# Linear attention into a top-1 mixture of experts on one core: five edits of a hand-written instruction order

## The chip, the cores and the metric

The kernel runs on one core of one Trainium2 chip. The metric is the device time of one execution in microseconds (us). Five engines take instructions from queues of their own, each in program order: TensorE (PE, with its weight loads shown apart as PEld), VectorE (DVE), ScalarE (ACT), GpSimd (POOL) and SyncE (SP), which mostly issues DMAs. An engine waits on semaphores for what another engine or a DMA has made.

## The reference

What is computed, cut to its core (B=4, H=8, S=768, D=48; 3072 tokens of 384; 8 experts, F=1024):

```python
for t in range(S):                                    # per batch and head, state 48x48
    cur = einsum('bhd,bhe->bhde', u * k_t, v_t)
    y[:, :, t] = einsum('bhd,bhde->bhe', r_t, state + cur)
    state = w * state + einsum('bhd,bhe->bhde', k_t, v_t)
x = y as (3072, 384)
logits = x @ w_gate + modality_bias[modality_id]      # 384 x 8
e_idx = argmax(logits); gate_w = softmax(logits)[e_idx]
for e in range(8):
    out[e_idx == e] = gate_w * (relu(x[e_idx == e] @ w1[e]) @ w2[e])
```

Inputs and outputs are float32.

## The kernel before, in words

**Attention in 24 units.** The recurrence is computed in chunks of 128 tokens. A unit is one chunk of one batch: 6 chunks outside, 4 batches inside, so unit i+4 carries on the state of unit i. For a unit, with transposed (`rT`, `kT`) and plain (`r`, `k`, `v`) inputs, the engines do:

- VectorE: `kc` = kT times powers of the decay (`keys`, L400).
- GpSimd: `rc` = rT times powers (`decay`, L376), `rk` = rc*kc for the bonus term (`own_keys`, L393; from unit 14 on `ru` = r*k*u instead, L389 and L390), `kt` = k times its weight (`carry`, L383).
- TensorE: scores `psc` (L450), bonus (L414), values `py` (L478, L485, L513), new states `pst` (L496, L500). VectorE masks the scores into `at` (L456) and makes the diagonal part `dv` (L427).
- VectorE or ScalarE add the state up (`st`, L550, L552), and both make the token's row in two half-precision parts (L535, L562, L566). SyncE turns the row with a transposing DMA (`flip`, L571) for the router's matmuls.

In unit i, the keys, scores and carries of units ahead are made beside the values of unit i and the rows of unit i-1.

**Routing.** Units are routed in groups of four (later three and two). When a group's places are known, GpSimd writes each of its units' rows to the array `rows` in memory, sorted by expert, with an indirect DMA (`send`, L680, each with a tiny memset L679 ahead of it). Three groups are sent from units 13, 17 and 21, four DMAs in a stretch; the first group is sent one DMA at a time between other GpSimd work of unit 9.

**First expert slots inside the attention.** One expert is known ahead, and its rows are worked on in slots of 128 rows while the attention still runs. For slot k: `s_turn(k)` has SyncE load a row number into a register, read 128 sorted rows with a transposing DMA into one half of `mxT` (L1024) and their gate factors into `mt` (L1025); `s_up(k)` is 72 matmuls (L1037), `s_high` and `s_low` split the relu in two parts `hh` (ScalarE, L1041) and `hl` (VectorE, L1046), `s_down` is 16 matmuls on `hh` (L1111) and 8 on `hl` (L1116), `s_due` (VectorE, L1096) makes the row factors. The expert's weights stand as a coarse half `whi` and a fine half `wlo`; `fine(q)` (VectorE, L977) makes 1024 columns of `wlo`. L1111 takes four terms with `whi`, four with `wlo`, and so on; `fine(5)` makes the columns of the last three. The weights' two scales are undone by the product `wf` (`undo`, L963). Slot 0 goes up in unit 12 and down in unit 13, slot 5 goes up in unit 22, and slots 6 to 9 in the tail, which starts behind unit 22. After it a device loop takes the remaining expert jobs.

**What sets the order.** Nothing schedules this kernel: each engine runs in the order in which `run()` is written. `plan(i, f)` puts f at the end of unit i, `soon(i, f)` into its middle; `ahead`, `turns` and `ups` are tables by unit; `route(i, d, f)` calls f for a group whose last unit was i-d. `first` holds for the units of the first form, up to unit 11.

Of the kernel before, what the change touches and what calls it, by code (L numbers as in the profile page):

```python
# [14 lines left out]
AF = mybir.ActivationFunctionType  # L15
# [4 lines left out]
B, H, S, D = 4, 8, 768, 48  # L20
# [46 lines left out]
class _Kernel:  # L67
# [16 lines left out]
    def setup(self):  # L84

        nc, c = self.nc, self.c
# [103 lines left out]
        self.scores(1)  # L190
        self.causal(0, 0)
        self.causal(0, 1)
        self.carry(0)
        self.own_keys(1)
        self.decay(2)
        pst = self.ps_s.tile([P, 512], F32, tag="s", name="psd")
        self.bonus(0, pst)
# [776 lines left out]
    def fine(self, q, part=0, parts=1):  # L974

        sl, sc = self.piece(q, part, parts)
        self.nc.vector.scalar_tensor_tensor(self.wlo[:, sl], self.raw[:, sl], sc, self.whi[:, sl], ALU.mult, ALU.subtract)  # L977
# [146 lines left out]
    def run(self):  # L1124
        nc, tc, m = self.nc, self.tc, self.m
# [25 lines left out]
        def plan(step, f):  # L1151
            at.setdefault(step, []).append(f)

        def piece(e, q, after=None):
            if q == 0:
                self.eid = nc.sync.value_load(self.ctl[:, e : e + 1], min_val=0, max_val=E - 1)
            self.load(self.eid, NQ, q, after=after)
# [3 lines left out]
        def scales(key, half, step, then=lambda: None):  # L1161
            def ask():
                begun[key] = self.scales_(key, slice(half, half + 1), self.ps_a, "big")
                next(begun[key])

            self.amid.setdefault(step, []).append(ask)
            plan(step, lambda: (run(begun[key], 9), then()))

        def chain(*gs):
            for g in gs:  # L1170
                yield from g
# [14 lines left out]
        fine = lambda q: lambda: self.fine(q)  # L1186
# [10 lines left out]
            plan(i, second(q))  # L1197
            plan(i + 3, norm(q))
        scales("w1", 0, 6)
        scales("w2", 1, 10, self.undo)  # L1200
        for q, i in enumerate((7, 8, 9)):
            soon(i, wide(q))
            plan(i, fine(q))
# [2 lines left out]
        plan(11, fine(3))  # L1206
        plan(12, wide(5))
        plan(12, fine(4))
        plan(12, fine(5))
        ahead = {0: (0, 1), 4: (2, 3), 8: (4, 5), 12: (6, 7), 16: (8,), 19: (9,)}  # L1210
        turns = {10: (0,), 11: (1,), 14: (2,), 15: (3,), 18: (4,), 19: (5,), 22: (6,)}
        ups = {12: 0, 14: 1, 16: 2, 18: 3, 20: 4, 22: 5}
        live = lambda i: 0 <= i < NU

        def route(i, d, f, *args):
            for lo, hi in GROUPS:
                if hi - 1 + d == i and lo in groups:
                    f(groups[lo], *args)

        def each(i, *fs):  # L1220
            for f in fs:
                if live(i):
                    f(i)


        def fill(n=1):
            if n < 99:
                n = min(n, quota.get(i, n))
                if i in quota:
                    quota[i] -= n  # L1230
            while n and fills:
                g = fills.pop(0)
                if next(g, fills) is not fills:
                    fills.append(g)
                    n -= 1

        quota = {1: 6, 2: 6, 3: 4}
        for i in range(NU - 1):
            if i > NEAR:
                each(i + 4, self.lines)  # L1240
            if i:
                each(i + 1, self.scores)
            if 0 <= i - 2 <= TURNED:
                self.flip(i - 2, False)
            route(i, 3, lambda u: fills.append(self.choose(u)))
            route(i, 5, lambda u: fills.append(chain(self.place(u), self.ahead(ahead[u["lo"]], u["pr"]))))
            up, down = ups.get(i), ups.get(i - 1)
            if down is not None:
                self.s_high(down, 0)
            first = i <= BARE  # L1250
            self.token(i - 1) if i else None
            for j in range(2 if first else 0):
                each(i - 1, lambda i: self.state(i, j))
                fill()
            if first:
                for f in early.get(i, ()):
                    f()
                gate = self.taken(i)
                if i <= NEAR:
                    self.lines(i + 3, gate if i else None)  # L1260
                fill()
            if first:
                each(i + 2, self.keys)
                for _ in self.factor(i - 1) if i else ():
                    fill()
                gate = self.causal(i + 1, 0)
                if i <= NEAR:
                    self.turned(i + 4, gate if i else None)
                fill()
                each(i - 1, self.high)  # L1270
                if 0 <= i - 2 <= TURNED:
                    self.flipped(i - 2)
                if i <= NEAR:
                    self.other(i + 4)
                else:
                    self.turned(i + 5, both=True)
                each(i + 1, lambda i: self.causal(i, 1))
                fill()
                gate = self.low(i - 1) if i else None
                for q in first_at.get(i, ()):  # L1280
                    piece(0, q, gate)
            if down is not None:
                self.s_high(down, 1)
            if ups.get(i - 2) is not None:
                self.s_take(ups[i - 2])
            if i and i - 1 == self.grp["lo"]:
                groups[i - 1] = self.grp
            fill()
            each(i, self.taken) if not first else None
            for j in range(0 if first else 2):  # L1290
                each(i - 1, lambda i: self.state(i, j))
                fill()
            for f in () if first else early.get(i, ()):
                f()
            if down is not None:
                self.s_low(down, 0)
                self.s_low(down, 1)
                self.s_due(down)
            late = i >= NU - 3
            if not first:  # L1300
                each(i + 2, self.keys)
                each(i + 5, lambda i: self.turned(i, both=True))
            for f in (lambda: each(i + 2, self.own_keys), lambda: each(i + 3, self.decay), lambda: None):
                if first:
                    route(i, 6, self.send, 1, True)
                f()
            if ups.get(i - 2) is not None:
                self.s_give(ups[i - 2])
            if not first:
                route(i, 6, self.send, B, True)  # L1310
            each(i + 2, self.carry)
            if first:
                route(i, 6, self.send, 1, True)
            route(i, 4, self.sign)
            if not first:
                for _ in self.factor(i - 1):
                    fill()
                self.own(i, 0)
                each(i - 1, self.high)
                for j in range(2):  # L1320
                    each(i + 1, lambda i: self.causal(i, j))
                    fill()
                self.own(i, 1)
                each(i - 1, self.low)
                fill()
            if i - 1 > TURNED:
                self.flip(i - 1)
            if i == NEAR:
                self.lines(i + 4)
                self.turned(i + 5, both=True)  # L1330
            fill()
            self.values(i)
            for g in range(2):
                if up is not None:
                    self.s_up(up, g)
                if down is not None:
                    self.s_down(down, g)
            for p in range(2):
                for h in range(2):
                    c, r = divmod(i + 1 - 2 * p - h, B)  # L1340
                    if r == 0 and 0 < c < NCH - 1 and not self.early(c):
                        self.fade(c, slice(2 * p, 2 * p + 2), range(2 * h, 2 * h + 2))
            if any(hi - 1 + d == i for lo, hi in GROUPS for d in (4, 5)):
                fill(99)
            route(i, 2, self.logits)
            route(i, 4, self.count)
            if late:
                route(i, 5, self.send, B, True)
            for f in at.get(i, ()):
                f()  # L1350
            for k in turns.get(i, ()):
                self.s_turn(k)
# [3 lines left out]
        i, j = NU - 2, NU - 1  # L1356
# [241 lines left out]
```

## Time and profile before

| | |
|---|---|
| median of 3 runs | 357.91 us (351.15, 357.91, 361.53) |
| profiled execution | 350.87 us, its span 349.0 us, mean granted TensorE clock 0.984 of full speed |
| PE, PEld | busy 328.6 us (94% of the span), 262.3 us (75%) |
| DVE | 222.6 us (64%) |
| ACT | 161.7 us (46%) |
| POOL | 168.0 us (48%) |
| memory | 50.29 MB in DMA packets, mean 144 GB/s |

The span runs from the first to the last instruction; 350.87 - 349.0 = 1.87 us lie around it. PE is busy nearly all the time, and POOL's 48% is an average: it is close to full in the first half of the span and nearly empty in the second. Times in the rows further down are microseconds from the span's start.

### The profile page before, as it was taken

The page shows a single profiled execution, that of the slowest core. Times are in us where ns is not written, and L with a number is a line of the kernel's source. Part 1 is how long each engine was busy: PE and PEld are TensorE (multiplying, and loading weights), DVE is VectorE, ACT ScalarE, POOL GpSimd, SP SyncE. Part 2 cuts the span into 40 slices and gives each one's busy share as a digit, 9 for nine tenths or more (in the row PEclk, how much of TensorE's full clock was granted, in tenths as well). Part 3 has the DMA queues.
Part 4 walks back from the last instruction along what each step waited for, and adds up shares of the span by engine and source line. Part 5 has one row for each costly group of instructions (what it writes and reads, how often), then busy time and mean ns, then how long its engine had stood idle before and what let it go on. Part 6 is the DMA issues. An engine that isn't in the chain of part 4 may idle for free. (4 is left out here: it accounts for less than half of the span.)

```text
span 349.0 us, 14765 instructions
## 1 busy us (share of the span) xinstructions
PE 328.6 (94%) x5387; PEld 262.3 (75%) x5387; DVE 222.6 (64%) x744; ACT 161.7 (46%) x379; POOL 168.0 (48%) x251
## 2 busy tenths in 40 slices
PE   7899999989898989998799999999999999999992
PEld 3687878779696959786778777777788888777771
DVE  6879688999786948696635863349333344337950
ACT  5756676755364547456433432256222222226920
POOL 8897688779985988375421631111111211111311
PEclk9989999999999998999899999999999999999999
DMA  7978989778999997814578541117832112111110
GB/s 136 268 177 237 238 233 243 211 208 169 269 237 186 253 255 149 182 50 139 130 158 258 198 115 48 45 45 220 214 67 46 45 45 65 48 45 45 36 45 5
DMA packets 51773, 50.29 MB, mean 144 GB/s; under 512 B 39176, under 2 KB 44041, under 8 KB 51472
## 3 DMA queue, kind: packets, MB, share of 16 engines
q1 hardware_dynamic: 47568, 37.45, 48.0%
q0 software_dynamic: 3200, 9.47, 7.9%
q10 hardware_dynamic: 960, 2.75, 3.1%
q8 instruction: 31, 0.51, 0.6%
q14 instruction: 14, 0.11, 0.1%
HBM read 30.55 MB, written 11.63 MB: 121 GB/s over the span
## 5 line engine op out<-in xcount | busy, mean ns | idle before, releaser
L1037 PEld LDWEIGHTS <-whi 128*128 128x128 f16 x1248 | 73.1, 98 | 5.2 <-DMA mxT<-rows 2.3
L1111 PEld LDWEIGHTS <-hh 128*128 128x128 f16 x416 | 38.4, 98 | 28.2 <-ACT hh L1041 3.5
L1037 PE MATMUL phb<-mxT,whi 128*128 128x128 f16 x720 | 47.5, 219 | 0.0
L1041 ACT ACTIVATE hh<-phb 128x256 f16<-128x256 f32 (+1 forms) x45 | 20.4, 454 | 43.5 <-PE phb L1037 17.9
L1037 PEld LDWEIGHTS <-wlo 128*128 128x128 f16 x624 | 38.3, 99 | 0.0
L376 POOL TENSOR_TENSOR rc<-ud,powr 128x512 f32<-128x512 f32 (+1 forms) x27 | 33.0, 1230 | 3.0 <-DMA ud<-in_pd 2.7
L680 POOL DMA_INDIRECT rows<-row,posi x24 | 25.3, 1056 | 16.4 <-issue 10.6
L456 DVE TENSOR_TENSOR at<-psc,mask 128x512 f32<-128x512 f32 x48 | 31.5, 681 | 2.6 <-remote 2.6
L1037 PE MATMUL phs<-mxT,whi 128*128 128x128 f16 x480 | 31.1, 222 | 2.0 <-DMA mxT<-rows 2.0
L1046 DVE SCALAR_TENSOR_TENSOR hl<-phb,hh 128x256 f16<-128x256 f32 (+1 forms) x45 | 22.7, 512 | 14.6 <-ACTq L1540 7.3
L450 PE MATMUL psc<-rc,kc 48*64 48x128 f32 x768 | 29.3, 278 | 2.7 <-issue 2.0
L1116 PEld LDWEIGHTS <-hl 128*128 128x128 f16 x208 | 19.9, 98 | 15.6 <-issue 2.8
L1006 POOL TENSOR_TENSOR seenb<-otb,putb 128x1 int32<-128x1 int32 x15 | 3.7, 249 | 56.9 <-ACTq L1520 49.5
L485 PE MATMUL py<-kv,at 128*64 128x48 f32 x768 | 28.5, 227 | 0.9 <-issue 0.6
L1111 PE MATMUL po<-whi,hh 128*128 128x384 f16 x128 | 28.8, 327 | 0.1
L1111 PE MATMUL po<-wlo,hh 128*128 128x384 f16 x128 | 28.6, 326 | 0.1
L485 PEld LDWEIGHTS py<-kv,at 128*64 128x64 f32 x768 | 26.8, 144 | 1.7 <-issue 1.0
L562 ACT ACTIVATE row<-py,sx 128x384 f16<-128x384 f32 x24 | 14.0, 582 | 29.6 <-DVE sx L329 26.5
L1037 PE MATMUL phb<-mxT,wlo 128*128 128x128 f16 x360 | 27.4, 219 | 0.0
L450 PEld LDWEIGHTS psc<-rc,kc 48*64 48x64 f32 x768 | 22.0, 133 | 6.5 <-issue 3.0
L1116 PE MATMUL po<-whi,hl 128*128 128x384 f16 x128 | 23.4, 326 | 1.2 <-PEq L1594 1.1
L997 ACT ACTIVATE otb<-po,fac 128x384 f32<-128x384 f32 x15 | 8.7, 582 | 34.1 <-PE phb L1037 30.8
(273 smaller groups left out, 651.3 us busy)
## 6 DMA issues: line engine op xcount, KB each, us to landing
ud<-in_pd SPq DMA_DIRECT2D x34, 192.0 KB
raw<-in_w SPq DMA_DIRECT2D x12, 512.0 KB
kv<-in_pt SPq DMA_DIRECT2D x10, 576.0 KB
kv<-in_pt SPq DMA_DIRECT2D x14, 384.0 KB
raw<-in_w SPq DMA_DIRECT2D x2, 1536.0 KB, 7.4
ud<-in_pd ACTq DMA_DIRECT2D x14, 192.0 KB
rows<-pad SPq DMA_DIRECT2D x1, 1544.0 KB
rows<-row,posi POOLq DMA_INDIRECT x24, 4.0
```

The costliest lines, as they stand in the source:

```text
L376: nc.gpsimd.tensor_mul(u["rc"][:, s], u["rT"][:, s], self.powr[:, s])
L450: nc.tensor.matmul(u["ps"][j][s, pr * P : (pr + 1) * P], u["kc"][r, pr, s], u["rc"][r, pr, :], start=True, stop=True)
L456: return nc.vector.tensor_mul(u["at"][:, j * NPR : (j + 1) * NPR, :], u["ps"][j].rearrange("p (q t) -> p q t", q=NPR), self.mask.unsqueeze ...
L485: nc.tensor.matmul(py[t, sl], u["at"][:, j * NPR + pr, t], u["v"][:, sl], start=c == h == 0, stop=h == H - 1 and i >= JOINED, skip_group_c ...
L562: self.nc.scalar.activation(u["x16"][:, :DM], u["x"], AF.Copy, scale=u["g"]["sx"][:, b : b + 1])
L680: i = nc.gpsimd.indirect_dma_start(out=self.rows, out_offset=bass.IndirectOffsetOnAxis(ap=u["posi"][:, b : b + 1], axis=0), in_=u["row"][: ...
L997: self.nc.scalar.activation(ot, po[:, :DM], AF.Copy, scale=gf[:, t : t + 1])
L1037: self.nc.tensor.matmul(ph[:, q * P : (q + 1) * P], w[:, c0 : c0 + P], self.xT[:, xq, t * P : (t + 1) * P], start=i == q == 0, stop=i == l ...
L1041: self.nc.scalar.activation(self.hh[:, f0 : f0 + fb, t * P : (t + 1) * P], p3, AF.Relu)
L1046: self.nc.vector.scalar_tensor_tensor(self.hl[:, f0 : f0 + fb, r], p3, 0.0, self.hh[:, f0 : f0 + fb, r], ALU.max, ALU.subtract)
L1111: self.nc.tensor.matmul(po[:, :DM], self.hh[:, f, t * P : (t + 1) * P], w[:, c0 : c0 + DM], start=n == 0, stop=False)
L1116: self.nc.tensor.matmul(po[:, :DM], self.hl[:, f, t * P : (t + 1) * P], self.whi[:, c0 : c0 + DM], start=False, stop=f == FB - 1)
```

## The change

Five edits of the order; what is computed stays the same.

1. In the setup `own_keys(1)` comes ahead of `carry(0)`.
2. The product `wf` at the end of unit 10 is made by ScalarE (an activation with a scale) instead of VectorE. The same product for later experts stays with VectorE.
3. `fine(5)` moves from the end of unit 12 to unit 13, behind `s_low(0)` and `s_due(0)`.
4. In the units of the second form the four sends of a group come behind `own_keys` and ahead of `decay`, instead of behind `decay`. In units of the first form the order stays.
5. `s_turn(6)` is called at the end of unit 21 instead of unit 22.

```diff
@@ setup
         self.causal(0, 1)
+        self.own_keys(1)
         self.carry(0)
-        self.own_keys(1)
         self.decay(2)
@@ run()
         scales("w1", 0, 6)
-        scales("w2", 1, 10, self.undo)
+        scales("w2", 1, 10, lambda: nc.scalar.activation(self.wf, self.winv[:, 0:1], AF.Copy, scale=self.winv[:, 1:2]))
...
         plan(12, fine(4))
-        plan(12, fine(5))
...
-        turns = {10: (0,), 11: (1,), 14: (2,), 15: (3,), 18: (4,), 19: (5,), 22: (6,)}
+        turns = {10: (0,), 11: (1,), 14: (2,), 15: (3,), 18: (4,), 19: (5,), 21: (6,)}
...
                 self.s_due(down)
+                if down == 0:
+                    fine(5)()
...
-            for f in (lambda: each(i + 2, self.own_keys), lambda: each(i + 3, self.decay), lambda: None):
-                if first:
-                    route(i, 6, self.send, 1, True)
-                f()
+            if first:
+                route(i, 6, self.send, 1, True)
+            each(i + 2, self.own_keys)
+            route(i, 6, self.send, 1 if first else B, True)
+            each(i + 3, self.decay)
             if ups.get(i - 2) is not None:
                 self.s_give(ups[i - 2])
-            if not first:
-                route(i, 6, self.send, B, True)
+            if first:
+                route(i, 6, self.send, 1, True)
             each(i + 2, self.carry)
```

On GpSimd at the end of the setup (`rk` of unit 1, `kt` of unit 0, then `rc` of unit 2 and `kt` of unit 1):

```order
 L182 TENSOR_TENSOR uw<-w,uT 48x4 x2
+L393 TENSOR_TENSOR rk_274<-rc_198,kc_196 128x512
 L383 TENSOR_TENSOR kt_89<-kv_111,wtok 128x384
-L393 TENSOR_TENSOR rk_275<-rc_198,kc_196 128x512
 L376 TENSOR_TENSOR rc_277<-ud_87,powr 128x512
 L383 TENSOR_TENSOR kt_90<-kv_114,wtok 128x384
```

The product for unit 1's bonus now stands ahead of the one that uses `kv`, a tile of unit 0's plain inputs.

On VectorE at the end of unit 12 and in unit 13 (the second `wlo` piece is `fine(5)`; `dv`, `st`, `hl` are unit 12's and slot 0's):

```order
 L814 TENSOR_TENSOR lim<-pr_1418,steps 128x2
-L977 SCALAR_TENSOR_TENSOR wlo<-raw,ws,whi 128x1024 x2
+L977 SCALAR_TENSOR_TENSOR wlo<-raw,ws,whi 128x1024
 L520 TENSOR_TENSOR py_1780<-py_1780,dv_1746 128x384
...
 L1096 TENSOR_SCALAR fac<-mt_301,wf 128x1
 L1097 TENSOR_TENSOR ids<-mt_301,skip 128x1
+L977 SCALAR_TENSOR_TENSOR wlo<-raw,ws,whi 128x1024
 L400 TENSOR_TENSOR kc_1945<-ud_88,powk 128x512
```

The piece moved past `py`, `dv`, two state updates and slot 0's relu, and stands ahead of unit 15's keys.

On SyncE at the end of units 21 and 22 (the three transposes are the flips of units 19, 20 and 21; `ctl` is read for slot 6):

```order
-L571 DMA_TRANSPOSE xT_3131<-row_3130 128x6x128 x3
+L571 DMA_TRANSPOSE xT_3131<-row_3130 128x6x128 x2
 L1068 TENSOR_LOAD ctl
 L1068 ISA x2
...
 L1025 ISA
 L1025 DMA mt_301<-rows 128x4
+L571 DMA_TRANSPOSE xT_3131<-row_3130 128x6x128
 L1068 TENSOR_LOAD ctl
 L1068 ISA x2
```

The load of slot 6's rows now stands ahead of unit 21's flip instead of behind it.

## Rows read from the trace of the kernel before

**Rows 1.** Waits of TensorE: what, for what; us in total, times, longest us.

```profile
PE phs L1037 <- DMA mxT<-rows: 2.0, 1, 2.0
PE psc L450 <- issue: 2.0, 3, 1.0
```

**Rows 2.** Stretches: us; busy us of PE, PEld, DVE, ACT, POOL; granted clock; DMA.

```profile
17.30:20.40 3.10, 3.10 (x50) 2.28 (x48) 2.27 (x9) 1.61 (x4) 3.10 (x3) 0.50 1.00 220
80.00:100.00 20.00, 18.51 (x402) 16.12 (x399) 17.36 (x52) 8.54 (x21) 17.99 (x21) 1.00 1.06 238
129.98:133.20 3.22, 3.22 (x55) 2.91 (x49) 3.13 (x13) 1.60 (x5) 2.83 (x3) 0.50 1.05 284
170.96:174.83 3.87, 3.87 (x47) 3.67 (x46) 2.82 (x12) 0.58 (x1) 3.37 (x18) 0.56 0.71 204
```

**Rows 3.** GpSimd at the setup's end: start, us, operation [idle before, releaser].

```profile
11.90 1.01 POOL L383 TENSOR_TENSOR kt<-kv,wtok 128x384 f32<-128x384 f32 x1 [1.32 <-DMA kv<-in_pt]
12.87 1.72 POOL L393 TENSOR_TENSOR rk<-rc,kc 128x512 f32<-128x512 f32 x1
14.55 1.26 POOL L376 TENSOR_TENSOR rc<-ud,powr 128x512 f32<-128x512 f32 x1
```

**Rows 4.** VectorE and TensorE in the same stretch.

```profile
7.87 0.69 DVE L400 TENSOR_TENSOR kc<-ud,powk 128x512 f32<-128x512 f32 x1 [0.60 <-DMA ud<-in_pd]
12.59 0.86 DVE L400 TENSOR_TENSOR kc<-ud,powk 128x512 f32<-128x512 f32 x1 [0.21 <-DMA ud<-in_pd]
13.47 0.56 PE L500 MATMUL pst<-kv,kt 128*48 128x48 f32 x16
14.64 0.63 PE L414 MATMUL pst<-uw,rk 112*64 112x2 f32 x16 [0.61 <-POOL rk L393]
15.86 1.10 PE L450 MATMUL psc<-rc,kc 48*64 48x128 f32 x32 [0.59 <-POOL rc L376]
```

**Rows 5.** VectorE, GpSimd and TensorE in unit 10.

```profile
70.49 3.50 DVE L963 TENSOR_TENSOR wf<-winv 128x1 f32<-128x1 f32 x1
72.97 1.00 POOL L383 TENSOR_TENSOR kt<-kv,wtok 128x384 f32<-128x384 f32 x1
74.94 0.87 PE L513 MATMUL py<-dv,id 128*64 128x384 f32 x4 [0.54 <-DVE dv L427]
```

**Rows 6.** All of line 963: min/median/max ns, first and last start.

```profile
L963 DVE TENSOR_TENSOR wf<-winv x3: 159/161/3502, 70.5 to 327.8; 128x1 f32<-128x1 f32 x3
```

**Rows 7.** VectorE, GpSimd and TensorE in units 12 and 13.

```profile
84.72 3.28 DVE L977 SCALAR_TENSOR_TENSOR wlo<-raw,ws,whi 128x1024 f16<-128x1024 f32 x2
89.60 1.29 DVE L1046 SCALAR_TENSOR_TENSOR hl<-phs,hh 128x512 f16<-128x512 f32 x2
89.71 0.56 PE L500 MATMUL pst<-kv,kt 128*48 128x48 f32 x16 [0.81 <-DVE st L550]
90.34 0.81 PE L1111 MATMUL pos<-whi,hh 128*128 128x384 f16 x4
88.83 1.27 POOL L376 TENSOR_TENSOR rc<-ud,powr 128x512 f32<-128x512 f32 x1
94.16 0.96 POOL L680 DMA_INDIRECT rows<-row,posi  x1 [0.23 <-issue]
```

**Rows 8.** SyncE, GpSimd and TensorE from unit 21's sends to the tail.

```profile
158.44 7.94 SPq L571 DMA_TRANSPOSE xT<-row  x2
159.90 0.96 POOL L680 DMA_INDIRECT rows<-row,posi  x1 [0.23 <-issue]
167.52 1.24 SPq L1024 DMA_TRANSPOSE mxT<-rows  x1
170.46 2.35 PE L1037 MATMUL phs<-mxT,whi 128*128 128x128 f16 x24 [2.05 <-DMA mxT<-rows]
```

**Rows 9.** All of line 680, and how long its DMAs take to land.

```profile
L680 POOLq EVENT_SEMAPHORE  x4: 17/30/7572, 56.7 to 196.8; - x4
DMA to landing us min/median/max: 2.9/4.0/6.8
```

## The prediction

> **What bounds the kernel now.** TensorE is busy 328.6 of 349.0 us, so the first view is not who is busiest but what TensorE waits for. Its list of waits [rows 1] is headed by 2.0 us for the load of a slot's rows, and by 2.0 us in three pieces that stand under "issue", in which nothing that the profile shows was missing. The rest is a dozen waits under 1 us each. The timelines then say where four of them lie: two at the end of the setup [rows 4], one in unit 10 [rows 5], one in unit 13 [rows 7], and the 2.05 us at the start of the tail [rows 8]. The windows add what such an idle time does afterwards: behind three stands of TensorE there is a stretch in which it is busy all the time at a granted clock of 0.50 to 0.56, the lower of its two levels [rows 2]: 3.10 us at 0.50, 3.22 us at 0.50, 3.87 us at 0.56. Work that takes 3.87 us at 0.56 takes 3.87 x 0.56 = 2.17 us at full clock, so that stretch lost 1.70 us; the other two lost 1.55 and 1.61. In 80 to 100 us GpSimd is busy 17.99 of 20 us [rows 2]: there its queue has about 2.0 us of slack. Behind the attention it is nearly idle, and TensorE alone sets the end, so a wait of TensorE that goes is a gain in full unless something later takes it back.
>
> **Edit 1, the setup.** GpSimd sits idle for 1.32 us until 11.90, waiting for `kv` [rows 3]. `rk` of unit 1, now in front, needs no `kv`: its `kc` was done at 7.87 + 0.69 = 8.56 [rows 4]. It took 1.72 us beside a `kc` of VectorE that itself took 0.86 instead of 0.69; if the two are served one after the other, 0.46 of the 1.72 is the overlap (12.87 to 13.33, start of `rk` to near the end of that `kc`), and alone it takes 1.26. It fits the idle time: 10.58 to about 11.85. `kt` stays at 11.90 to 12.91, before TensorE uses it at 13.47. Then unit 2's `kc` (0.69) and `rc` (1.26) run one behind the other and end at 12.91 + 0.69 + 1.26 = 14.86, instead of 15.81. The bonus need not wait its 0.61 us, and the scores start at 14.85 instead of 15.86: **gain 1.01 us**. Bounds: if `kc` and `rc` overlap freely, 1.20; if VectorE's `kc` loses against three GpSimd products in a row, as in unit 10 below, scores no sooner and 0.2 us lost at the next masks, so -0.2. Of the clock stretch at 17.30 to 20.40 I take nothing in the forecast, because GpSimd stays only just ahead there; if the clock stays up, 1.55 us more.
>
> By the Trainium skill, page "SBUF — State Buffer", section "Who interferes with whom", a VectorE instruction with two inputs in SBUF and a GpSimd instruction that reads SBUF exclude each other for a whole instruction. The 1.72 beside 0.86 agrees [rows 3, 4]; by that rule the gain is 1.01, without it 1.20.
>
> **Edit 2, the product of scales.** VectorE's `wf` stood 3.50 us from 70.49 [rows 5]; the two other executions of the line took about 0.16 us [rows 6]. It ended only when GpSimd's third product in a row ended, at 72.97 + 1.00 = 73.97. TensorE then waited 0.54 us for `dv` behind it [rows 5]. On ScalarE the product takes about as little (0.16 is VectorE's own price; no row has ScalarE's), and what stands behind it there has slack of over 1 us. **Gain 0.54 us**; low end -0.1, if ScalarE's wait for the scales delays the row behind it. High end 0.54, since TensorE waited no longer. VectorE gets 3.3 us free; late next is unit 12's `kc`, which reads two tiles in SBUF as `wf` did and may stand in its place, but `dv` is ahead of it.
>
> By the same section of the Trainium skill the lock holds for the one instruction that has it. One GpSimd product (1.28 us) and the own 0.16 would make 1.44; 3.50 over three products speaks against that [rows 5], and the measurement decides. It is why I keep a starved `kc` among the rivals.
>
> **Edit 3, the last fine piece.** Two pieces took 3.28 us from 84.72 [rows 7], 1.64 each. TensorE's state matmuls waited 0.81 us for `st` at 88.9 to 89.71, behind them. Without the second piece `st` is there at about 89.57 - 1.64 = 87.9, ahead of TensorE: **gain 0.81 us**. The piece then starts behind slot 0's relu, which took 1.29 us from 89.60 [rows 7]. What stands ahead of that relu moves up by the same 1.64, so it can run from 87.96 to 89.25; with 0.2 us for two small instructions the piece runs from 89.5 to 91.1. The first matmul that wants it is the 14th of L1111; four of these take 0.65 us from one row to the next, 0.162 each; they start at 90.34 - 0.81 = 89.53 without the wait, and the 14th comes at 89.53 + 13 x 0.162 = 91.6. Half a microsecond to spare. Low end: if the relu doesn't come sooner, the piece ends at 89.60 + 1.29 + 0.2 + 1.64 = 92.7, 1.1 late, and the gain is -0.3. High end 0.81.
>
> **Edit 4, the sends.** At unit 13 `rc` stood at 88.83 to 90.10, the four sends behind it until 94.16 + 0.96 = 95.12 [rows 7]: 5.02 us. Now the sends start 1.27 us sooner and `rc` 5.02 us later. It is made three units ahead and its scores are computed one unit ahead, so it has about two units; from the state matmuls at 13.47 [rows 4] to those at 89.71 [rows 7] thirteen units pass, 5.9 us each, so 11.7 us of cover against 5.0. Nobody waits for rows sent 1.27 us sooner except slot 6's load (edit 5), and at unit 21 there is no `rc` left, so nothing moves there. **0 us**. What I can't price is the stands under "issue" that follow the sends of units 13, 17 and 21: 2.0 us in three pieces [rows 1] and 1.61 us of clock behind the longest. They may shrink or move with the sends: -1 to +1.6 us, taken as 0.
>
> **Edit 5, slot 6's rows.** The load started at 167.52 [rows 8], 1.14 us behind the end of the two flips at 158.44 + 7.94 = 166.38, and TensorE had its rows 170.46 - 167.52 = 2.94 us later. TensorE was free at 170.46 - 2.05 = 168.41. Asked for ahead of unit 21's flip, the load waits for the last of unit 21's sends: issued at 159.90, landing after 2.9, 4.0 or 6.8 us (least, median, most) [rows 9]. Rows are there 2.94 us behind that: at 165.7, 166.8 or 169.6. Wanted at 168.41, so at the median the wait of 2.05 is gone, and with it, I take it, the 1.70 us of low clock right behind it [rows 2]: **gain 3.75 us**. Low end: at 6.8 there is 1.2 us of wait and the low clock left, gain 0.8. Queued behind the waiting load on SyncE is unit 21's flip, up to 2 us later; the router wants it only behind slot 6's matmuls and unit 22's values.
>
> **Sum.** 1.01 + 0.54 + 0.81 + 0 + 3.75 = 6.11 us. Against the profiled execution's 350.87 that is 344.8 (-1.7%). That execution is as fast as the best of the three runs (351.15); their median is 357.91. For the time I start between the two, at 354.4: **348.3 us**.
>
> **Rivals.**
> 1. *More: the clock stays up at the start too.* TensorE reaches its first long stretch without the 1.2 us of waits [rows 4], and 1.55 us at 17.30 to 20.40 come on top: 343.2 (-2.2%). For it: the stretch lies right behind those waits. Against: some wait for GpSimd's next products remains.
> 2. *The load is asked sooner, but comes no sooner*, so that edit 5 doesn't do what it says: it waits for sends that land after 6.8 us. Sum 6.11 - 2.93 = 3.2, time 347.7 (-0.9%). For it: the slowest landing is in the trace [rows 9], and the memory is busy there. Against: the median.
> 3. *A starved `kc`* in the setup or in unit 12, as `wf` was: edit 1 at -0.2, time 346.0. GpSimd's products in a row speak for it, the 0.86 us of the `kc` at 12.59 against [rows 4].
> 4. *Slower: sends stand at the head of GpSimd's queue.* One stand of a send there took 7.57 us [rows 9]. If at units 13 and 17 the sends, now ahead, wait that long for something `rc` used to cover, `rc`, `kt` and `ru` stand behind them; with 2.0 us of slack each costs 5.6, and 1.6 of clock [rows 2]. 350.87 - 6.1 + 2 x 7.2 = 359.1 (+2.3%). It decides where the stand passes the slack. Against: the present sends start with only 0.15 to 0.23 us of idle time ahead of them, so they were ready.
>
> **How the numbers follow.** Chances: forecast 0.42, rival 1 0.28, rival 2 0.18, rival 3 0.07, rival 4 0.05. About 2%, 7 us, is what measurements of this kernel tell from no change, its three runs being 10 us apart. Faster by over 2%: rival 1 and the forecast's upper edge, 0.28 + 0.05 = 0.33; slower by over 2%: 0.05; within 2%: 0.62. The range: rival 1 with 1 us from the stands behind sends, 342; rival 2 from the runs' median, 357.91 - 3.2 = 354.7, with 1.3 of the stands, 356.
>
> **What would show it.** In the changed profile: the bonus at the setup's end starts without waiting, and the clock at 17 to 20 us tells forecast from rival 1; no 3.5 us instruction of VectorE in unit 10; the state matmuls in unit 13 without a wait, and no gap ahead of the 14th of L1111; slot 6's load ahead of unit 21's flip, its matmuls at about 166 us without a wait and at full clock. I am wrong if TensorE's waits go and the span doesn't shrink with them, if new stands under "issue" take their place, or if GpSimd shows a wait ahead of a send at unit 13 or 17.

## The result, and the profile after

The changed kernel took 352.22 us (median of 20 runs, 347.12 to 356.27) against 356.04 for the kernel before (20 runs, 351.06 to 361.53): **ratio 0.9891, 95% interval 0.9844 to 0.9938**, so 3.9 us faster (2.2 to 5.6) where 6.1 was forecast. The time lies inside the range of 342 to 356.

Ratios here are formed from the runs within 1.5% of the fastest of the same kernel, medians from all runs; the first profiled execution of the changed kernel (354.71 us, mean clock 0.966) lies outside, so the rows here are from a later one, the run `e1_all_again`: span 347.2 us, clock 0.989, against 349.0 and 0.984 before.

TensorE at the end of the setup and near 27 us (start, us, operation [idle before, releaser]):

```profile
13.90 0.63 PE L414 MATMUL pst<-uw,rk 112*64 112x2 f32 x16
14.73 1.10 PE L450 MATMUL psc<-rc,kc 48*64 48x128 f32 x32 [0.21 <-POOL rc L376]
...
24.18 1.22 PE L450 MATMUL psc<-rc,kc 48*64 48x128 f32 x32 [0.95 <-POOL kt L383]
26.41 0.33 PE L576 MATMUL pt<-id,row 128*128 128x128 f16 x3 [1.01 <-DVE at L456]
26.94 0.34 PE L576 MATMUL pt<-id,row 128*128 128x128 f16 x3 [0.20 <-DVE row0f L767]
```

The bonus no longer waits and unit 2's scores start at 14.73 instead of 15.86 [rows 4]; 14.85 was forecast. But 10 us later TensorE waits 0.95 us for GpSimd and 1.01 and 0.20 us for VectorE.

The product of scales, now on ScalarE, then SyncE around slot 6's load:

```profile
69.70 0.29 ACT L1200 ACTIVATE wf<-winv 128x1 f32<-128x1 f32 x1 [1.12 <-DVE winv L332]
```

```profile
146.98 9.75 SPq L571 DMA_TRANSPOSE xT<-row  x2
160.27 1.24 SPq L1024 DMA_TRANSPOSE mxT<-rows  x1
161.71 0.42 SPq L1025 DMA_DIRECT2D mt<-rows  x1
162.24 1.95 SPq L571 DMA_TRANSPOSE xT<-row  x1
```

The 3.50 us of VectorE [rows 5] are gone, and slot 6's load stands ahead of unit 21's flip. TensorE there:

```profile
165.30 0.22 PE L646 MATMUL pr<-oh,warm 128*128 128x8 f16 x3
165.38 1.50 PE L1037 MATMUL phs<-mxT,whi 128*128 128x128 f16 x24
...
169.99 0.34 PE L485 MATMUL py<-kv,at 128*64 128x48 f32 x4 [0.48 <-issue]
171.46 0.20 PE L485 MATMUL py<-kv,at 128*64 128x48 f32 x1 [1.14 <-issue]
171.59 1.15 PE L1111 MATMUL pos<-whi,hh 128*128 128x384 f16 x4
172.54 1.48 PE L1111 MATMUL pos<-wlo,hh 128*128 128x384 f16 x4
...
177.18 1.50 PE L1037 MATMUL phs<-mxT,whi 128*128 128x128 f16 x24
```

Slot 6's matmuls start at once, at full clock (24 in 1.50 us instead of 2.35 [rows 8]). Then come two stands, idle times of TensorE under "issue", of 0.48 and 1.14 us, which the first profile of the kernel before did not have, and low clock behind them: the eight L1111 shown end at 174.02, 2.4 us after their start, where full clock makes it 1.5 (four in 0.65 us [rows 7], the last ending 0.81 behind its row's start). Windows (us; busy of PE, PEld, DVE, ACT, POOL; clock; DMA) of the start, around unit 18 and of this stretch:

```profile
17.30:20.40 3.10, 3.10 (x76) 2.69 (x73) 2.92 (x13) 2.08 (x6) 3.10 (x3) 1.00 1.02 236
120.00:135.00 15.00, 14.16 (x242) 11.94 (x241) 10.27 (x33) 8.81 (x27) 13.43 (x18) 0.89 0.93 231
160.00:176.00 16.00, 13.98 (x206) 11.30 (x206) 9.99 (x36) 6.73 (x20) 4.47 (x20) 0.89 0.58 128
```

The clock at the start is 1.00 here, 0.50 in the kernel before [rows 2].

### The profile page after: what moved, and what is told of

The parts are those of the page before. It is cut to its first block, busy times and chain, and to the rows that moved or that the text cites. A ratio compares the mean times of both kernels' runs of the same rounds, so it can differ in the third digit from the quotient of the medians.

```text
span 351.9 us, 14762 instructions
## 1 busy us (share of the span) xinstructions
PE 331.9 (94%) x5387; PEld 265.1 (75%) x5387; DVE 220.9 (63%) x743; ACT 161.6 (46%) x380; POOL 165.8 (47%) x251
## 5 line engine op out<-in xcount | busy, mean ns | idle before, releaser
L1037 PEld LDWEIGHTS <-whi 128*128 128x128 f16 x1248 | 72.3, 98 | 5.4 <-issue 1.8
L1111 PEld LDWEIGHTS <-hh 128*128 128x128 f16 x416 | 38.5, 98 | 26.3 <-ACT hh L1041 3.1
L1037 PE MATMUL phb<-mxT,whi 128*128 128x128 f16 x720 | 47.5, 219 | 1.5 <-DVE mxT L1480 1.5
L1037 PEld LDWEIGHTS <-wlo 128*128 128x128 f16 x624 | 37.7, 98 | 0.5 <-issue 0.5
L376 POOL TENSOR_TENSOR rc<-ud,powr 128x512 f32<-128x512 f32 (+1 forms) x27 | 34.0, 1265 | 2.3 <-DMA ud<-in_pd 2.2
L485 PE MATMUL py<-kv,at 128*64 128x48 f32 x768 | 30.5, 232 | 2.8 <-issue 2.6
L1116 PEld LDWEIGHTS <-hl 128*128 128x128 f16 x208 | 19.9, 98 | 15.6 <-issue 2.8
L485 PEld LDWEIGHTS py<-kv,at 128*64 128x64 f32 x768 | 28.3, 148 | 4.0 <-issue 3.7
L1037 PE MATMUL phs<-mxT,whi 128*128 128x128 f16 x480 | 30.1, 219 | 0.7 <-DMA mxT<-rows 0.7
L1006 POOL TENSOR_TENSOR seenb<-otb,putb 128x1 int32<-128x1 int32 x15 | 2.9, 192 | 56.2 <-ACTq L1522 48.3
L1111 PE MATMUL po<-whi,hh 128*128 128x384 f16 x128 | 28.8, 327 | 0.0
L1111 PE MATMUL po<-wlo,hh 128*128 128x384 f16 x128 | 28.7, 326 | 0.0
L1037 PE MATMUL phb<-mxT,wlo 128*128 128x128 f16 x360 | 27.4, 219 | 0.0
L450 PEld LDWEIGHTS psc<-rc,kc 48*64 48x64 f32 x768 | 22.8, 141 | 4.2 <-POOL rc L376 1.9
```

The lines of the kernel that those rows point to most:

```text
L376: nc.gpsimd.tensor_mul(u["rc"][:, s], u["rT"][:, s], self.powr[:, s])
L450: nc.tensor.matmul(u["ps"][j][s, pr * P : (pr + 1) * P], u["kc"][r, pr, s], u["rc"][r, pr, :], start=True, stop=True)
L485: nc.tensor.matmul(py[t, sl], u["at"][:, j * NPR + pr, t], u["v"][:, sl], start=c == h == 0, stop=h == H - 1 and i >= JOINED, skip_group_c ...
L1037: self.nc.tensor.matmul(ph[:, q * P : (q + 1) * P], w[:, c0 : c0 + P], self.xT[:, xq, t * P : (t + 1) * P], start=i == q == 0, stop=i == l ...
L1111: self.nc.tensor.matmul(po[:, :DM], self.hh[:, f, t * P : (t + 1) * P], w[:, c0 : c0 + DM], start=n == 0, stop=False)
L1116: self.nc.tensor.matmul(po[:, :DM], self.hl[:, f, t * P : (t + 1) * P], self.whi[:, c0 : c0 + DM], start=False, stop=f == FB - 1)
```

## The experiments

Executions of one kernel lie 10 us and more apart, so edits worth 1 us don't show in a time. But TensorE runs the same instructions in the same order in every kernel here, so stretches of its timeline can be compared directly. Three are used:

- **S1**: from the span's start to the last three row transposes (L576) near 27 us.
- **S2**: from the first L1037 of slot 2 to the first of slot 3 (units 16 to 18, with unit 17's sends inside).
- **S3**: from the last router matmul ahead of slot 6 (L646) to the first L1037 of slot 6's second half (before: 168.20 to 179.80).

S1, S2 and S3 are each of one execution. The medians (us) are of all runs, of this kernel and of the kernel before on the same chip.

| kernel (edits in it) | ratio, 95% interval | medians | S1 | S2 | S3 |
|---|---|---|---|---|---|
| before (none) | | | 27.07 | 18.65 | 11.60 |
| e5_before_again (none) | one execution | 349.69 / 356.58 | 26.44 | 18.62 | 10.68 |
| e6_setup_only (1) | 1.0059, 0.9990 to 1.0129 | 354.75 / 356.58 | 26.96 | 16.80 | 12.02 |
| e10_wf_and_fine (2, 3) | 0.9960, 0.9850 to 1.0070 | 355.40 / 357.82 | 26.79 | 17.20 | 11.88 |
| e4_sends_only (4) | 0.9964, 0.9911 to 1.0016 | 353.67 / 357.31 | 27.17 | 16.18 | 11.83 |
| e2_load_only (5) | 1.0006, 0.9932 to 1.0080 | 357.03 / 357.31 | 27.06 | 19.54 | 12.01 |
| e3_without_load (1 to 4) | 1.0007, 0.9933 to 1.0081 | 356.30 / 357.31 | 27.68 | 16.16 | 11.88 |
| e9_without_sends (1, 2, 3, 5) | 1.0021, 0.9953 to 1.0088 | 354.85 / 357.82 | 26.14 | 18.68 | 10.27 |
| e7_without_setup (2 to 5) | 0.9974, 0.9873 to 1.0075 | 354.69 / 356.58 | 26.86 | 15.68 | 9.48 |
| changed, first profile (all) | 0.9891, 0.9844 to 0.9938 | 352.22 / 356.04 | 29.65 | 15.67 | 9.51 |
| e1_all_again (all) | 0.9880, 0.9816 to 0.9944 | 352.78 / 357.31 | 26.94 | 17.47 | 11.88 |
| e8_last_sends_late (all, tail's sends late) | one execution | 351.44 / 356.58 | 26.96 | 15.96 | 7.82 |
| e11_spread (all, sends spread) | **0.9824, 0.9717 to 0.9930** | 347.81 / 357.82 | 27.34 | 15.21 | 7.82 |
| e12_spread_only (none, sends spread) | 0.9969, 0.9918 to 1.0019 | 346.25 / 349.05 | 27.08 | 15.51 | 9.92 |

**The whole change again, and the load alone.** Edit: none; `22: (6,)` to `21: (6,)`.

> The changed kernel once more, for a profile beside others of the same chip. Theory A (the sum's terms are there, but part is given back): 3 to 5 us below the kernel before, the waits of the setup, of dv, of st and of slot 6 gone, and instead new stands of TensorE under "issue" at the places where it loads instructions, with a low clock behind them. Rival B (the terms themselves were smaller than read): no more stand time under "issue" than the 4 to 5 us of the kernel before, and the waits that should be gone partly there.

> The kernel before with edit 5 alone: slot 6's rows asked for in unit 21. Forecast of the prediction: the wait of 2.05 us and the low clock behind it go, 3.75 us faster (ratio 0.989). Rival (the load waits for the sends): 0.8 us or less, ratio 0.998, and a wait of about 1.2 us left ahead of slot 6's matmuls.

The first, at 0.988, is inside theory A's 3 to 5 us. Its list of waits has 7.0 us under "issue" (seven lines, 2.5 to 0.4 us), against 5.4 in the first profile of the kernel before; but that sum can't tell A from B, since e5, the kernel before unchanged, has 8.3. For the second, 1.0006 excludes the forecast's 0.989. Its wait for slot 6 is gone entirely, so the rival falls too: four stands of 0.19 to 0.48 us and a low clock behind them ate the gain within the same stretch (S3 12.01).

**Without the load, and the sends alone.** Edit: the whole change with `22: (6,)`; the loop around `self.send` alone.

> The changed kernel without edit 5 (edits 1 to 4 alone). By the sum 2.4 us faster than the kernel before (ratio 0.993), with slot 6's wait of about 2 us still there. If edits 1 to 4 give their gains back in stands elsewhere: 0 to 1 us, ratio 0.997 to 1.000; if edit 5 is worth less than forecast, as fast as the whole change.

> The kernel before with edit 4 alone: sends ahead of rc in units 13 and 17. Forecast: no change in time (within 1 us), rc 5 us later and unnoticed. Rival (the sends disturb TensorE where they now lie): 1 to 3 us slower, with stands of TensorE beside the sends of units 13 and 17 that are longer than the 0.62 and 1.33 us of the kernel before.

Without the load the ratio is 1.0007: nothing is left of the 2.4 us that the sum gives edits 1 to 4, though the interval reaches down to 0.9933. So neither the load nor the other four edits show a gain alone, and together they show 1.1%; intervals of 0.7% to each side just leave room for that. The sends alone come out at 0.9964; the rival (slower by 1 us or more) lies outside the interval, and S2 is 2.5 us shorter than before.

**The kernel before again.** Edit: none.

> The kernel before, unchanged, for a second profile of it. Theory A (the prediction read waits that only that one execution had): the waits of 0.54 us for dv in unit 10 and of 0.81 us for st in unit 13 are not both there, while the stands under "issue" lie at the same instructions as in the first profile with other lengths. Rival B (they belong to the kernel): both waits again, within 0.3 us of the first profile.

Its waits of TensorE (us in total, times, longest) and VectorE's product of scales:

```profile
PE psc L450 <- issue: 4.7, 5, 1.8
...
PE pt L576 <- DVE at L456: 1.0, 1, 1.0
PE psc L450 <- POOL rc L376: 1.0, 1, 1.0
PE phs L1037 <- DVE posi L662: 0.9, 1, 0.9
```

```profile
71.48 1.27 DVE L963 TENSOR_TENSOR wf<-winv 128x1 f32<-128x1 f32 x1
```

Neither the wait for `dv` nor the one for `st` is there: theory A. `wf` took 1.27 us instead of 3.50 [rows 5], and slot 6 waited 0.91 us instead of 2.05. Of the six profiles without edit 2, two (before, e6) have the wait for `dv`, and of the six without edit 3 the same two the one for `st`. `wf` itself is slow in all six, 1.27 to 3.50 us; it mostly cost TensorE nothing.

In the setup e5's scores start at 14.90 us, without edit 1 and behind the 1.0 us of waiting for `rc` above. In its tail, where slot 6 waits less, stands follow at unit 23's values, without edit 5:

```profile
169.85 1.51 PE L1037 MATMUL phs<-mxT,whi 128*128 128x128 f16 x24 [0.91 <-DVE posi L662]
...
173.33 0.34 PE L485 MATMUL py<-kv,at 128*64 128x48 f32 x3 [0.28 <-issue]
174.09 0.34 PE L485 MATMUL py<-kv,at 128*64 128x48 f32 x5 [0.42 <-issue]
```

**The setup alone, and all but the setup.** Edit: `own_keys(1)` ahead of `carry(0)`, alone or left out.

> The kernel before with edit 1 alone. Forecast of the prediction: 1.0 us faster, ratio 0.997, unit 2's scores about 1 us sooner and the lead kept. Theory A (given back): the scores come sooner, but a TensorE that is ahead reaches its next instruction loads before these are done, so that unit 4 is reached no sooner than in the kernel before (28.7 us from the span's start), and the time is the same within 1 us or up to 1.5 us longer.

> The changed kernel without edit 1. By the sum 5.1 us faster than the kernel before (ratio 0.986) and 1 us slower than the whole change. If edit 1 gives its gain back and more: as fast as the whole change or 1 us faster (0.985 to 0.988).

e6's interval, from 0.9990, leaves out the forecast of 0.997, but the medians of all its runs give 0.995: the times don't decide. Its TensorE rows, scores first:

```profile
14.80 1.10 PE L450 MATMUL psc<-rc,kc 48*64 48x128 f32 x32 [0.18 <-POOL rc L376]
...
26.43 0.33 PE L576 MATMUL pt<-id,row 128*128 128x128 f16 x3 [1.02 <-DVE at L456]
26.96 0.34 PE L576 MATMUL pt<-id,row 128*128 128x128 f16 x3 [0.20 <-DVE row0f L767]
```

At 14.80 the scores are sooner than the first profile's 15.86, and level with e5's 14.90; at 26.96 (27.07 before) nothing is left. Given back, as theory A has it, but to VectorE's masks and row, not to an instruction load. Leaving the edit out gave 0.9974, above both expectations (0.985 to 0.988), whose upper edge its interval just reaches. Its S2 and S3 are those of the whole change or better; why its times are worse stays open.

**The tail's sends later.** Edit:

```diff
         self.s_down(5, 1)
-        self.send(g4, B, True)
...
         self.s_give(5)
+        self.send(g4, B, True)
```

> The changed kernel with the tail's three sends some 10 us later on GpSimd (behind slot 5's give). Theory C (the sends beside an instruction load make the stands of TensorE behind slot 6): the stands of 0.9 to 1.6 us at unit 23's values are gone, slot 6 to slot 5's down part takes 2.5 us instead of 4.2 to 5.5; slot 8 waits for its rows instead, about 4 us. Rival D (the stands come from the instruction load alone, whatever else runs): the stands stay, 0.9 us or more.

```profile
167.59 1.50 PE L1037 MATMUL phs<-mxT,whi 128*128 128x128 f16 x24
...
170.40 1.09 PE L485 MATMUL py<-kv,at 128*64 128x48 f32 x32
171.42 0.82 PE L1111 MATMUL pos<-whi,hh 128*128 128x384 f16 x4
...
175.33 1.50 PE L1037 MATMUL phs<-mxT,whi 128*128 128x128 f16 x24
188.75 1.44 PE L1037 MATMUL phs<-mxT,whi 128*128 128x128 f16 x23 [1.92 <-DMA mxT<-rows]
```

Theory C: unit 23's 32 L485 run without a stand in 1.09 us, and S3 is 7.82. Slot 8 waits for its rows instead, 1.92 us rather than 4. The three sends still stand in a row, from 178.34 us on, but now beside the expert's matmuls, and there they make no stand: TensorE is busy for all 10.00 us from 176 to 186.

**Without the sends' move, and edits 2 and 3 alone.** Edit: the old loop around `self.send` in the changed kernel; `wf` and `fine(5)` alone.

> The changed kernel without edit 4: sends behind rc again in units 13 and 17. Forecast of the prediction: as fast as the whole change (edit 4 at 0). Theory A (edit 4 is worth something, because the sends lie where TensorE doesn't stand for them): 1.5 to 2.5 us slower than the whole change, ratio to the kernel before 0.993 to 0.996, and two stands together of 1.0 to 1.4 us at unit 18's scores, beside the sends of unit 17, as in both profiles of the kernel before.

> The kernel before with edits 2 and 3 alone. Forecast of the prediction: 1.35 us faster, ratio 0.996. Theory A (their waits stand in two of five executions only): 0.5 us faster, ratio 0.998 to 1.000, which these rounds can't tell from no change; no wait for dv in unit 10 nor for st in unit 13 in the profile.

e9 beside unit 17's sends (GpSimd 124.27 to 129.08):

```profile
128.69 0.41 PE L450 MATMUL psc<-rc,kc 48*64 48x128 f32 x2 [0.36 <-issue]
130.10 1.38 PE L450 MATMUL psc<-rc,kc 48*64 48x128 f32 x18 [0.99 <-issue]
131.40 1.55 PE L478 MATMUL py<-st,rc 112*64 112x96 f32 x16
```

Stands and low clock (16 L478 in 1.55 us, at full clock in e4 0.88) as before, S2 at 18.68: theory A. The time is 4.7 us worse than the whole change by the two ratios, more than the 1.5 to 2.5 of theory A, with intervals of 0.5 and 0.7% to each side; by the medians it is 0.9 us worse (0.9917 against 0.9893). e10's time can't tell; neither wait is in its profile.

**Sends spread.** Edit (the two calls around `carry` lose their `if first` as well; in the tail the three sends stand ahead of `setup3`, behind it and behind the two `sign`):

```diff
-            if first:
-                route(i, 6, self.send, 1, True)
+            route(i, 6, self.send, 1, True)
             each(i + 2, self.own_keys)
-            route(i, 6, self.send, 1 if first else B, True)
+            route(i, 6, self.send, 1, True)
             each(i + 3, self.decay)
...
```

> The changed kernel with the sends of units 13, 17, 21 and of the tail one at a time between GpSimd's other work, instead of three or four in a row. Theory C (several sends in a row make TensorE's small stands, 0.4 to 1.4 us at each of the four places): these stands shrink by half or more, 1.5 to 3 us faster than the whole change, ratio to the kernel before 0.980 to 0.985. Rival D (the stands come whatever the spacing): as fast as the whole change, 0.988, with stands of the same sum.

> The kernel before with the spread sends of the run e11_spread and none of the five edits. Theory C (the stands beside several sends in a row are the largest loss that an order can mend): 4 to 6 us faster than the kernel before (ratio 0.984 to 0.989), with the stands at units 14, 18 and 22 at half or less, and slot 6's wait of about 2 us still there. Rival D (the spread pays only together with slot 6's sooner load, since the tail's stands come with that): 0 to 2 us faster (0.995 to 1.000).

e11's waits of TensorE, and the tail's stretch in its windows:

```profile
PE pst L500 <- issue: 3.1, 1, 3.1
PE py L485 <- issue: 2.2, 2, 1.5
...
PE psc L450 <- issue: 1.0, 3, 0.4
```

```profile
160.00:176.00 16.00, 16.00 (x295) 14.06 (x288) 11.04 (x44) 10.49 (x32) 6.22 (x25) 1.00 0.61 128
```

With 0.9824 e11 is clear of the kernel before. Whether it also beats the changed kernel (0.9891) isn't shown: the intervals overlap. No stand is left in the tail's stretch. The two large ones (3.1 and 1.5) are of another kind (last section). Spread without the five edits was a miss for theory C: 0.9969 where it said 0.984 to 0.989, and where D said 0.995 to 1.000. Its stands at the sends are gone too (S2 15.51), and slot 6's wait is there (S3 9.92, 2.1 over e11):

```profile
165.39 1.51 PE L1037 MATMUL phs<-mxT,whi 128*128 128x128 f16 x24 [1.94 <-DMA mxT<-rows]
```

Behind this wait of 1.94 us the matmuls run at full clock (24 in 1.51 us), where behind the 2.05 of the kernel before they took 2.35 [rows 8]. That chip was faster (before: 349.05), and the profile has two other stands of 2.1 us each. Why the spread alone gained so little stays open.

## Why the prediction was right and where it was wrong

Right: the sign, "within 2%" as the likeliest, the range; all four waits that were to go went (0.21 us is left of edit 1's two). Wrong were the sizes: of the priced terms none came in full, and one priced at nothing is there. The prediction's own sign of being wrong, new stands under "issue" in place of the waits, came too. The forecast time of 348.3 was 3.9 us low: 1.6 because the kernel before, put at 354.4, measured 356.04, and 2.3 because the change gave 3.8 (by the medians) and not 6.1. That the total is no further off is in part luck, since terms missed in both directions.

- **Edit 5 was mis-sized: 3.75 forecast, about 1.0 measured.** S3 averages 11.65 us (10.68 to 12.02) in the six kernels that have neither edit 5 nor spread sends, 10.63 (9.48 to 12.01) in the five with edit 5 and the tail's sends in a row. What failed is the step "with it, I take it, the 1.70 us of low clock". TensorE, 2 us ahead, now came to unit 23's values while GpSimd's three sends ran, and stood there; in e1 and e2 it got its low clock there. The old wait had covered those sends: in e5, where it was only 0.91 us, three stands of 0.28 to 0.42 us lie there without edit 5. With the sends out of the way (e8, e11) S3 is 7.82, 3.8 less, as much as the forecast; but in e12 the low clock is gone while the wait is there, so as far as one profile shows it went with the sends' place and not with the load. Beside spread sends the load is worth 2.1 us, not much more than its wait.
- **Edit 1: 1.01 forecast, none measured.** The scores came as forecast, at 14.73, but 15.86 was a late execution of the kernel before: without edit 1 they start at 14.88 to 15.86 in seven profiles, with it at 14.38 to 15.08. The other step that failed is the one not taken: what is late next. The last three row transposes wait for VectorE at 26.1 to 27.7 us in every profile but the changed kernel's first, with edit 1 (median 26.96) or without (27.06). The clock at the start, rival 1, changes between executions of one kernel: 17.30 to 20.40 ran at 1.00 in e1 and at 0.55 in the first profile after, at 0.50 in the kernel before and at 1.00 in e5.
- **Edits 2 and 3: 0.54 and 0.81 forecast; there in two of six executions each**, so 0.2 and 0.3 us on average, an estimate. The step took one execution's waits for the kernel's. The late end that was feared for `fine(5)` didn't come. By the Trainium skill, page "SBUF — State Buffer", section "Who interferes with whom", the lock that starves `wf` lasts one instruction. The rows don't agree: as the 3.50 us of rows 5 outlast three GpSimd products, e5's 1.27 us (71.48 to 72.75) outlast the end of one, at 71.76, and the whole of the next, which ends at 72.72.
- **Edit 4: 0 forecast; 2.1 us measured at unit 17, none at unit 13.** S2 is 18.25 us on average (16.80 to 19.54) in the six kernels without it and 16.19 (15.67 to 17.47) in the six with it. It was called unpriceable and given -1 to +1.6; "taken as 0" failed for these sends. They start sooner and end before TensorE comes to unit 18's scores, and the stands shrink: 0.29 and 0.55 us in e1, ahead of these scores, none beside the sends in e4, against 0.36 and 0.99 at the scores in e9. The like stretch around unit 13's sends, from the first L1037 of slot 0 to the first of slot 1, shows no gain: 17.8 us without edit 4 and 18.1 with it, single ones from 15.6 to 21.1. That `rc` comes 5 us later nobody noticed, as forecast; rival 4 didn't come: in the changed kernel's first profile no send of units 13 and 17 waited more than 0.22 us.

Measured sum: 1.0 + 0 + 0.5 + 2.1 - 0.3 = 3.3, against 3.9 by the times. Each of these is an average over a few executions that scatter by 1 to 2 us and more, so the agreement is no proof of the parts. The times don't bear the parts out either: each kernel with one of the edits 1, 4 and 5 left out lies 0.8 to 1.3% over the whole change, together more than the whole gained. Where in the program the 3.9 us come from is thus shown only in part. That the stands in S3 come from the tail's sends is shown by e8 and e11, which move these and lose the stands; by what path a send holds TensorE up is not.

## What to carry to other kernels

A wait that goes is a gain only if the next meeting of the engines moves too: follow the engine that gains to its next wait, and ask what the old wait had covered. Look at two or three executions of the kernel before an edit is priced at a few tenths of a microsecond. Where TensorE sets the end, look at what it does beside several indirect DMAs in a row on GpSimd: here it stood beside them in the matmuls of the attention and the router and not in the expert's, and other work between the DMAs, or another place for them, took the stands away.

## What the runs showed of the hardware that was not expected

**TensorE stands where its own instructions are loaded.** For these matmuls of unit 11 the profile shows no data that was missing, and in 12 of the 14 profiles TensorE stands ahead of them. The kernel before, the changed kernel's first profile, and e11:

```profile
77.10 0.51 PE L500 MATMUL pst<-kv,kt 128*48 128x48 f32 x13 [0.59 <-issue]
```

```profile
79.29 0.79 PE L500 MATMUL pst<-kv,kt 128*48 128x48 f32 x13 [2.49 <-issue]
```

```profile
78.69 0.79 PE L500 MATMUL pst<-kv,kt 128*48 128x48 f32 x13 [3.10 <-issue]
```

The DMA queue for instructions had one load of 16 KB starting in the windows 74.2 to 74.6, 76.6 to 76.75 and 76.1 to 76.25 us of these three, about 2.6 us ahead of each end. In the changed kernel's first profile:

```profile
q8 instruction: 1, 0.02, 54.8%
```

In all twelve the load starts 2.4 to 2.9 us ahead of the stand's end, while the stand is 0.22 to 3.10 us long. So its length goes with when the load starts; that the load is the cause is read from this, and no run changed it. How much of the distance between executions of one kernel comes from such stands isn't shown. The Trainium skill, page "Runtime: NRT & Kernel Launch", section "Instruction fetch mechanics", calls the cost of passing from one 16 KB block to the next mostly hidden. By number the traces agree: of some 31 such loads in an execution, at most 8 have a stand of TensorE ending 2.0 to 3.1 us after their start. At this place the load was not hidden.

**Beside GpSimd's sends the stands are of another form:** several of 0.2 to 0.5 us close together. Unit 22's values have them in all twelve profiles with four sends in a row at unit 21, and in neither of the two with spread sends.
